# Six edits to an ordered one-core kernel: loaded keys, another bank for a scale, earlier state adds, later settling, blank rows behind a relu

## The chip, the cores and the metric

The kernel runs on one core of a Trainium2 chip. The metric is the device time in microseconds of one execution, as the median of several runs. A core has TensorE (PE, matrix products), VectorE (DVE), ScalarE (ACT), GpSimd (POOL) and SyncE (SP), each with a queue of its own in program order, and 16 DMA engines that move data between DRAM and the on-chip memory. On-chip data lie in SBUF; TensorE writes into the banks of PSUM.

## The reference

An attention with a decaying state, whose output rows go through a layer of experts. B, H, S, D = 4, 8, 768, 48; the layer has 3072 tokens of width 384, 8 experts and a hidden width of 1024.

```python
for t in range(S):
    kt, vt, rt = k[:, :, t], v[:, :, t], r[:, :, t]
    cur = einsum('bhd,bhe->bhde', u[None] * kt, vt)
    y[:, :, t] = einsum('bhd,bhde->bhe', rt, state + cur)
    state = w[None, :, :, None] * state + einsum('bhd,bhe->bhde', kt, vt)
x = y.transpose(0, 2, 1, 3).reshape(B * S, H * D)

logits = x @ w_gate + modality_bias[modality_id]
e_idx = argmax(logits, axis=1)
probs = softmax(logits)
for e in range(8):
    mask = e_idx == e
    h = maximum(x[mask] @ w1[e], 0)
    out[mask] = probs[mask, e] * (h @ w2[e])
```

## The kernel before

**Units and steps.** The sequence is cut into 6 chunks of 128 tokens; a chunk of one batch is a unit, 24 in all. Step i of a loop computes the scores of unit i+1, the values of unit i and the tail of unit i-1 (its scaling, its split into two float16 halves, its transposition). The order of every engine's instructions is the order in which the program emits them: nothing reorders them later, so a line that is moved in `run` moves its instructions on each engine that they use.

**One unit.** `turned` loads the transposed receptance of a unit into a tile `ud`, and its transposed keys behind it unless the unit is in `TURNED`; `lines` loads keys and values by rows into `kv`. For units of `TURNED`, `keys_turned` makes the transposed keys on TensorE, with four transposes into a PSUM bank `pkT`. `decay` (GpSimd, `rc`) and `keys` (VectorE, `kc`) multiply both by powers of the decay. `scores` multiplies kc by rc into two banks, `causal` masks these into `at`, and `values` writes the unit's output into the bank `py` and its new state into the bank `pst`. Also in `pst` stands the bonus of the next unit: `taken` copies it out (`d`), and `own` multiplies it by the values (`dv`, eight ScalarE instructions in two halves, `own(i, 0)` and `own(i, 1)`). `add` adds dv to the output, and `token` does this and squares the sum on ScalarE. `state` adds the bank's new state to the decayed state in SBUF (two VectorE adds); the decay itself is `fade` on ScalarE, or for units 4 to 13 a matmul with a diagonal matrix, L497, and two copies by `settled_state`. From step `EASED` = 15 on, VectorE does `taken`; units from 17 on are in `OWNED` and take their bonus by a VectorE reduction over products instead.

**Routing.** Tokens are routed by groups of units, (0,4), (4,8), (8,12), (12,16), (16,19), (19,22), (22,24). For each there are `logits` (a PSUM bank `pr`), `choose`, `count`, `place`, and `send`, which writes token rows to DRAM by expert. `choose`, `place` and `ahead` (the numbers of the next early blocks, called settling below) are generators: they wait in a list `fills`, and `fill()` emits one small operation, `fill(99)` all that are left. `route(i, d, f)` calls f for the group whose last unit is i - d; `SOON` = 8 parts the first two groups from the later ones.

**Early expert blocks.** The weights of the expert that comes first are loaded during steps 8 and on; `norm` squares a sixth on ScalarE, and `scales` sums the squares with a small matmul into a free corner of some bank and works out a power of two. Nine blocks of 128 rows (slots 0 to 8) of this expert run between the steps and after them: `s_turn` reads the rows transposed from DRAM, `s_up`, `s_high`, `s_low`, `s_down` are the two layers with the relu between them, `s_take` and `s_give` write the result out. Behind them the job part takes the other blocks one after another: `turn` reads a block's rows transposed into `mxT` (or `xn`, from which VectorE copies), `up` is the first layer.

**Blank rows.** `pads` writes 128 blank rows behind an expert's rows, at a place that SyncE first loads into a register, one write of 193 KB for each. `pace` makes SyncE load a value and so wait until it is there.

Of the kernel before, what the change touches and what calls it, by code (L numbers as in the profile page):

```python
# [19 lines left out]
B, H, S, D = 4, 8, 768, 48  # L20
# [3 lines left out]
DM = H * D  # L24
# [3 lines left out]
FB = F // P  # L28
# [15 lines left out]
DENSE = 6  # L44
FADED = range(4, 14)
SHARED = range(9, 14)
TURNED = range(1, 15)
RAISED = range(6, 12)
OWNED = range(17, 24)
GROUPED = 6  # L50
EASED = 15
# [4 lines left out]
SOON = 8  # L56
GROUPS = ((0, 4), (4, 8), (8, 12), (12, 16), (16, 19), (19, 22), (22, 24))
# [10 lines left out]
class _Kernel:  # L68
# [260 lines left out]
    def turned(self, i):  # L329
# [3 lines left out]
        ud = self.ud[i % len(self.ud)]  # L333
        m = n if i in TURNED else 2 * n
        self.nc.sync.dma_start(ud[LOW:TOP, :m], self.pd[b * NCH + c].rearrange("j d n -> (j d) n")[:, :m])
# [12 lines left out]
    def keys_turned(self, i):  # L348

        if i in TURNED:  # L350
            u = self.ctx_[i]
# [620 lines left out]
    def norm(self, junk, q):  # L972
        self.nc.scalar.activation(junk, self.raw[:, q * WQ : (q + 1) * WQ], AF.Square, accum_out=self.ssq[:, q : q + 1])
# [191 lines left out]
    def run(self):  # L1165
# [22 lines left out]
        groups = {}  # L1188
        fills = []
        at, begin, mid = {}, {}, {}  # L1190

        def plan(step, f):
            at.setdefault(step, []).append(f)
# [12 lines left out]
        def scales(key, q, bank):  # L1206
            for _ in self.scales_(key, slice(q, q + 1), bank):
                pass
# [15 lines left out]
        O = GROUPS[0][1] + 4  # L1224
# [7 lines left out]
            plan(O + 9 + q, norm(q))  # L1232
        for q in range(3):
            plan(O - 1 + q, norm(q))
        begin[O + 2] = lambda: scales("w1", 0, self.ctx_[O + 1]["py"][:, DM + H :])
        for q in range(3):
            plan(O + 2 + q, wide(q))
            plan(O + 2 + q, norm(3 + q))
# [9 lines left out]
        def route(i, d, f, *args):  # L1248
            for lo, hi in GROUPS:
                if hi - 1 + d == i and lo in groups:  # L1250
                    f(groups[lo], *args)

        def each(i, *fs):
            for f in fs:
                if live(i):
                    f(i)


        def fill(n=1):
            while n and fills:  # L1260
                g = fills.pop(0)
                if next(g, fills) is not fills:
                    fills.append(g)
                    n -= 1

        for i in range(NU - 1):
# [27 lines left out]
            if i and i < EASED:  # L1294
                self.taken(i)
                self.shared(i)
            self.token(i - 1) if i else None
            if ups.get(i - 2) is not None:
                self.s_take(ups[i - 2])
# [2 lines left out]
            if i >= EASED:  # L1302
                self.taken(i)
                self.shared(i)
                for j in range(2):
                    self.state(i - 1, j)
            fill()
            if 0 < i < NU - 5:
                self.pace(self.ctx_[i]["d"])
                each(i + 5, self.turned)  # L1310
# [38 lines left out]
            if i - 2 in RAISED:  # L1349
                self.flipped(i - 2)  # L1350
            mid.get(i, lambda: None)()
            for j in range(2):
                each(i + 1, lambda i: self.causal(i, j))
                if j == 0:
                    each(i - 1, self.low)
                fill()
            self.own(i, 1)
            if late:
                for d in (6, 7):
                    route(i, d, lambda u: (self.rest(self.ctx_[i]["dv"][:1, DM - 1 :]), self.send(u, 1)))  # L1360
# [22 lines left out]
            if down is not None:  # L1383
                self.s_down(down, 0)
                self.s_down(down, 1)
            if i != O + 4 and any(hi - 1 + d == i for lo, hi in GROUPS for d in (4, 5)):
                fill(99)
            route(i, 2, lambda u: u["lo"] >= SOON and self.logits(u))
            route(i, 4, lambda u: u["lo"] >= SOON and self.count(u))
# [8 lines left out]
        i, j = NU - 2, NU - 1  # L1398
# [79 lines left out]
        self.s_low(7, 0)  # L1478
        self.s_up(7, 1)

        self.pads(*range(E - 2))
        self.turn(0, self.s_row(NE), m2, group="first")
        self.pads(E - 2, E - 1)
        self.s_high(7, 1)
        run(jobs, 5)
        self.s_low(7, 1)
        run(jobs, 4)
# [119 lines left out]
```

## Time and profile before

| | us |
|---|---|
| median of 3 runs | 337.85 |
| lowest, highest | 337.64, 340.84 |
| profiled execution | 340.3 |
| its span | 338.0 |

The span goes from the first to the last instruction of the profiled execution, and the execution's own time is 2.3 us longer. TensorE's granted clock is 0.996 of full speed over the span. Busy time is counted by engine; a matmul's weight load (PEld) runs beside other matmuls. In the trace steps 3 to 22 begin on TensorE with their scores; step 8 at 46.31, step 9 at 51.95, step 10 at 56.98, step 13 at 75.43, step 15 at 93.08, step 17 at 109.51. The job part begins at 192.58.

### The profile page before, as it was taken

To read this page: it belongs to the slowest core of one execution; us is meant where nothing else is said; L and a number is where in the kernel's file an instruction comes from. 1 tells how busy PE (TensorE), PEld (TensorE's weight loads), DVE (VectorE), ACT (ScalarE), POOL (GpSimd) and SP (SyncE) were. 2 spreads that over 40 slices of the span, in tenths; PEclk is the share of its full clock that TensorE was granted. 3 is DMA by queue.
4 is the path that set the end of the run, shared out by engine and by line. 5 is a ranking of instruction groups with operands and counts; after the bars stand their busy time and mean duration, and the time that the engine had idled before them with its cause. 6 is when DMAs were issued, how large, how long until landed. Compare 5 with 4: busy or idle time off the path is not lost. (4 is left out here: it accounts for less than half of the span.)

```text
span 338.0 us, 15234 instructions
## 1 busy us (share of the span) xinstructions
PE 320.1 (95%) x5450; PEld 263.6 (78%) x5450; DVE 213.7 (63%) x727; ACT 181.5 (54%) x500; POOL 160.5 (47%) x241
## 2 busy tenths in 40 slices
PE   6998999999999999999998999999999999999993
PEld 3787989888787879698876788886888777777771
DVE  7879867899989887976685423386333332333950
ACT  7898689899465757567411222274222225542920
POOL 8978764997489857562557112103111111111211
PEclk9999999999999999999999999999999999999998
DMA  6799797995499999964336532119622111122120
GB/s 187 238 162 185 140 234 227 337 233 173 72 215 239 275 244 303 268 107 120 93 113 239 124 70 47 47 47 327 121 64 53 47 47 23 47 64 53 37 47 5
DMA packets 58014, 47.93 MB, mean 142 GB/s; under 512 B 42345, under 2 KB 50808, under 8 KB 57713
## 3 DMA queue, kind: packets, MB, share of 16 engines
q1 hardware_dynamic: 54768, 37.85, 50.2%
q0 software_dynamic: 3200, 9.47, 7.6%
q8 instruction: 30, 0.49, 0.6%
q14 instruction: 16, 0.12, 0.1%
HBM read 27.21 MB, written 11.83 MB: 116 GB/s over the span
## 5 line engine op out<-in xcount | busy, mean ns | idle before, releaser
L1067 PEld LDWEIGHTS <-whi 128*128 128x128 f16 x1248 | 72.6, 98 | 3.2
L1076 DVE SCALAR_TENSOR_TENSOR hl<-phb,hh 128x256 f16<-128x256 f32 (+1 forms) x48 | 24.6, 512 | 68.8 <-issue 39.2
L1130 PEld LDWEIGHTS <-hh 128*128 128x128 f16 x416 | 39.0, 98 | 29.1 <-ACT hh L1071 3.5
L1067 PE MATMUL phb<-mxT,whi 128*128 128x128 f16 x768 | 50.9, 219 | 0.0
L1071 ACT ACTIVATE hh<-phb 128x256 f16<-128x256 f32 (+1 forms) x48 | 21.5, 455 | 40.6 <-PE phb L1067 21.0
L438 ACT ACTIVATE dv<-kv,d 128x48 f32<-128x48 f32 x172 | 42.9, 324 | 0.0
L1067 PEld LDWEIGHTS <-wlo 128*128 128x128 f16 x624 | 37.7, 98 | 0.0
L1036 POOL TENSOR_TENSOR seenb<-otb,putb 128x1 int32<-128x1 int32 x16 | 4.1, 256 | 64.8 <-ACTq L1538 51.7
L458 DVE TENSOR_TENSOR at<-psc,mask 128x512 f32<-128x512 f32 x48 | 32.5, 682 | 1.0 <-PE psc L452 0.9
L1130 PEld LDWEIGHTS <-hl 128*128 128x128 f16 x208 | 19.8, 98 | 15.7 <-issue 2.5
L366 POOL TENSOR_TENSOR rc<-ud,powr 112x512 f32<-112x512 f32 (+1 forms) x25 | 30.9, 1240 | 0.2
L1130 PE MATMUL po<-whi,hh 128*128 128x384 f16 x136 | 27.7, 326 | 2.0 <-ACT hh L1071 1.2
L1067 PE MATMUL phb<-mxT,wlo 128*128 128x128 f16 x384 | 29.3, 219 | 0.0
L701 POOL DMA_INDIRECT rows<-row,posi x24 | 24.6, 1024 | 9.8 <-issue 3.4
L452 PE MATMUL psc<-rc,kc 64*64 64x128 f32 (+1 forms) x768 | 27.9, 276 | 1.4 <-POOL rc L366 1.1
L1130 PE MATMUL po<-whi,hl 128*128 128x384 f16 x136 | 28.0, 326 | 1.2 <-PEq L1603 0.7
L1130 PE MATMUL po<-wlo,hh 128*128 128x384 f16 x136 | 27.7, 326 | 0.0
L1027 ACT ACTIVATE otb<-po,fac 128x384 f32<-128x384 f32 x16 | 9.3, 580 | 34.0 <-PE phb L1067 31.4
L1067 PE MATMUL phs<-mxT,whi 128*128 128x128 f16 x432 | 27.1, 219 | 0.1
L489 PE MATMUL py<-kv,at 128*64 128x48 f32 x768 | 26.6, 222 | 0.0
L489 PEld LDWEIGHTS py<-kv,at 128*64 128x64 f32 x768 | 25.2, 138 | 0.8 <-issue 0.5
L1009 DVE SCALAR_TENSOR_TENSOR wlo<-raw,ws,whi 128x1024 f16<-128x1024 f32 (+1 forms) x20 | 24.9, 1269 | 1.2 <-issue 0.7
(294 smaller groups left out, 623.0 us busy)
## 6 DMA issues: line engine op xcount, KB each, us to landing
kv<-in_pt SPq DMA_DIRECT2D x21, 384.0 KB
ud<-in_pd SPq DMA_DIRECT2D x10, 384.0 KB
raw<-in_w SPq DMA_DIRECT2D x12, 256.0 KB
raw<-in_w SPq DMA_DIRECT2D x6, 512.0 KB
raw<-in_w SPq DMA_DIRECT2D x2, 1536.0 KB, 7.1
ud<-in_pd SPq DMA_DIRECT2D x14, 192.0 KB
rows<-pad SPq DMA_DIRECT2D x10, 193.0 KB
rt<-in_pt SPq DMA_DIRECT2D x7, 192.0 KB
```

What stands on the lines that cost most here:

```text
L366: nc.gpsimd.tensor_mul(u["rc"][:TOP, s], u["rT"][:TOP, s], self.powr[:TOP, s])
L438: nc.scalar.activation(u["dv"][:, sl], u["v"][:, sl], AF.Copy, scale=u["d"][:, h : h + 1])
L452: nc.tensor.matmul(u["ps"][j][s, pr * P : (pr + 1) * P], u["kc"][r, pr, s], u["rc"][r, pr, :], start=True, stop=True)
L458: nc.vector.tensor_mul(u["at"][:, j * NPR : (j + 1) * NPR, :], u["ps"][j].rearrange("p (q t) -> p q t", q=NPR), self.mask.unsqueeze(1).to_ ...
L489: nc.tensor.matmul(py[t, sl], u["at"][:, j * NPR + pr, t], u["v"][:, sl], start=c == h == 0, stop=h == H - 1, skip_group_check=True)
L701: i = nc.gpsimd.indirect_dma_start(out=self.rows, out_offset=bass.IndirectOffsetOnAxis(ap=u["posi"][:, b : b + 1], axis=0), in_=u["row"][: ...
L1009: self.nc.vector.scalar_tensor_tensor(self.wlo[:, sl], self.raw[:, sl], sc, self.whi[:, sl], ALU.mult, ALU.subtract)
L1027: self.nc.scalar.activation(ot, po[:, :DM], AF.Copy, scale=gf[:, t : t + 1])
L1067: self.nc.tensor.matmul(ph[:, q * P : (q + 1) * P], w[:, c0 : c0 + P], self.xT[:, xq, t * P : (t + 1) * P], start=i == q == 0, stop=i == l ...
L1071: self.nc.scalar.activation(self.hh[:, f0 : f0 + fb, t * P : (t + 1) * P], p3, AF.Relu)
L1076: self.nc.vector.scalar_tensor_tensor(self.hl[:, f0 : f0 + fb, r], p3, 0.0, self.hh[:, f0 : f0 + fb, r], ALU.max, ALU.subtract)
L1130: self.nc.tensor.matmul(po[:, :DM], h[:, f, t * P : (t + 1) * P], w[:, c0 : c0 + DM], start=first, stop=last)
```

## The change

- Units 8 to 11 leave `TURNED`: their transposed keys come by DMA with the receptance, and TensorE doesn't transpose them.
- The first scale's matmul (before step 10's second half) writes into columns 480 and on of the second group's `pr`, not into unit 9's `py`.
- From step 15 on the state's adds are emitted ahead of `token`, `taken` and what stands between.
- What `fills` still holds for the groups from unit 8 on is emitted in the first half of steps 17 and 21, behind `fill()`, no longer at the ends of steps 16 and 20.
- `own(i, 1)` is emitted ahead of the masks, no longer behind them.
- The seventh slot's second relu is emitted ahead of seven of the blank rows' eight writes and of the job part's first transposing read, as is a `pace` on its result. (`pads(E)`, one more write, stays where it was.)

```diff
-TURNED = range(1, 15)
+TURNED = (*range(1, 8), *range(12, 15))
...
-        begin[O + 2] = lambda: scales("w1", 0, self.ctx_[O + 1]["py"][:, DM + H :])
+        begin[O + 2] = lambda: scales("w1", 0, groups[B]["pr"][:, 480:])
...
             if i and i < EASED:
                 self.taken(i)
                 self.shared(i)
+            if i >= EASED:
+                for j in range(2):
+                    self.state(i - 1, j)
             self.token(i - 1) if i else None
...
             if i >= EASED:
                 self.taken(i)
                 self.shared(i)
-                for j in range(2):
-                    self.state(i - 1, j)
             fill()
+            route(i, 6, lambda u: u["lo"] >= SOON and fill(99))
...
             mid.get(i, lambda: None)()
+            self.own(i, 1)
             for j in range(2):
                 each(i + 1, lambda i: self.causal(i, j))
                 if j == 0:
                     each(i - 1, self.low)
                 fill()
-            self.own(i, 1)
...
-            if i != O + 4 and any(hi - 1 + d == i for lo, hi in GROUPS for d in (4, 5)):
+            if i != O + 4 and any(hi - 1 + d == i for lo, hi in GROUPS for d in ((4,) if lo >= SOON else (4, 5))):
                 fill(99)
...
+        self.s_high(7, 1)
+        self.pace(self.hh[:, FB // 2, :2])
         self.pads(*range(E - 2))
         self.turn(0, self.s_row(NE), m2, group="first")
         self.pads(E - 2, E - 1)
-        self.s_high(7, 1)
```

## Rows read from the trace of the kernel before

**Rows 1.** The page, busy time, share of the span and instructions of each engine.

```profile
PE 320.1 (95%) x5450; PEld 263.6 (78%) x5450; DVE 213.7 (63%) x727; ACT 181.5 (54%) x500; POOL 160.5 (47%) x241
```

**Rows 2.** Busy time by stretch; last columns granted clock, DMA share, GB/s.

```profile
48.29:60.65 12.36, 11.82 (x317) 10.96 (x316) 8.97 (x33) 12.21 (x41) 7.13 (x8) 1.00 0.84 274
...
46.00:55.00 9.00, 8.81 (x234) 8.12 (x233) 7.28 (x21) 8.14 (x26) 4.74 (x4) 1.00 1.06 268
75.43:85.42 9.99, 9.43 (x233) 9.01 (x231) 9.78 (x27) 9.70 (x21) 7.23 (x8) 1.00 0.70 185
```

**Rows 3.** Timeline of TensorE in step 7: start, us, engine, line, operation.

```profile
42.65 0.65 PE L354 MATMUL pkT<-id,kv 128*112 128x128 f32 x4
...
43.23 0.88 PE L482 MATMUL py<-st,rc 112*64 112x96 f32 x16
```

**Rows 4.** Timeline of ScalarE and TensorE, steps 8 and 9; idle time before in brackets.

```profile
48.29 1.06 ACT L973 ACTIVATE junk<-raw 128x1024 f16<-128x1024 f32 x1 [0.51 <-DMA raw<-in_w]
...
55.18 0.17 ACT L421 COPY d<-pst 128x8 f32<-128x8 f32 x1
...
55.53 0.57 PE L497 MATMUL pst<-st,wd 112*64 112x48 f32 x15
```

**Rows 5.** Groups by line and form, the decayed keys: busy us, mean ns.

```profile
L404 DVE TENSOR_TENSOR kc<-pkT,powk 112x512 f32<-112x512 f32 x14 | 9.6, 682 | 0.8 <-PE pkT L354 0.8
...
L404 DVE TENSOR_TENSOR kc<-ud,powk 112x512 f32<-112x512 f32 x9 | 7.9, 882 | 0.0
```

**Rows 6.** DMA issues, the loads of transposed keys and receptance.

```profile
ud<-in_pd SPq DMA_DIRECT2D x10, 384.0 KB
...
ud<-in_pd SPq DMA_DIRECT2D x14, 192.0 KB
```

**Rows 7.** Timeline around the first scale, step 10.

```profile
60.42 0.17 DVE L613 TENSOR_SCALAR pr<-sx 128x4 int32<-128x4 int32 x1 [0.28 <-PE pr L600]
60.45 0.20 ACT L529 ACTIVATION_READ_ACCUMULATOR row<-py 128x1 f32 x1
...
60.69 0.17 PE L988 MATMUL py<-wssq,onesb 128*128 128x3 bf16 x1 [0.58 <-ACT row L529]
```

**Rows 8.** Timeline of step 15: fade, state, and the next state's matmuls.

```profile
94.95 0.79 ACT L470 ACTIVATE st<-st,w 112x192 f32<-112x192 f32 x2
...
95.77 0.72 DVE L542 TENSOR_TENSOR st<-st,pst 64x192 f32<-64x192 f32 x2
...
96.63 0.64 PE L502 MATMUL pst<-kv,kt 128*64 128x48 f32 x16 [0.58 <-DVE st L542]
```

**Rows 9.** Timeline of step 17: last settling operation, state, the next state's matmuls.

```profile
111.19 0.15 DVE L831 TENSOR_SCALAR skip<-again 128x1 int32<-128x1 f32 x1
...
112.20 0.71 DVE L542 TENSOR_TENSOR st<-st,pst 64x192 f32<-64x192 f32 x2
...
113.06 0.64 PE L502 MATMUL pst<-kv,kt 128*64 128x48 f32 x16 [0.71 <-DVE st L542]
```

**Rows 10.** Timeline of the seventh slot's second half, and the job part's first matmuls.

```profile
178.38 0.83 PE L1067 MATMUL phs<-mxT,wlo 128*128 128x128 f16 x12
...
181.00 0.60 ACT L1071 ACTIVATE hh<-phs 128x512 f16<-128x512 f32 x1 [3.12 <-remote]
...
181.65 0.82 PE L1130 MATMUL pos<-whi,hh 128*128 128x384 f16 x4 [1.14 <-ACT hh L1071]
...
192.58 0.61 PE L1067 MATMUL pha<-mxT,whi 128*128 128x128 f16 x8
```

**Rows 11.** Timeline of SyncE's DMA queue: blank rows and first transposing read.

```profile
177.00 8.13 SPq L959 DMA_DIRECT2D rows<-pad  x7
187.46 1.26 SPq L1054 DMA_TRANSPOSE mxT<-rows  x1
```

**Rows 12.** Timeline: the next transposing read, and VectorE's copy of what it brought.

```profile
194.07 1.23 SPq L1054 DMA_TRANSPOSE xn<-rows  x1
...
197.69 0.36 DVE L1516 COPY mxT<-xn 128x768 f16<-128x768 f16 x1
```

## The prediction

> **What bounds the kernel now.** I read the page's busy times first, then the busy time by stretch, and then, for each edit, the timeline and the waits at its own place. TensorE is busy for 320.1 of 338.0 us [rows 1], so nothing that another engine saves counts unless TensorE waited for it. The rest of its time lies in short waits of 0.5 to 1.2 us, and each of the six edits can be held against one of them, or against none. In the stretch that the first edit touches the other engines are full as well: from 48.29 to 60.65 ScalarE is busy for 12.21 of 12.36 us, in step 13 VectorE for 9.78 and ScalarE for 9.70 of 9.99, and the DMA engines' share is 1.06 in 46 to 55 and 0.84 from 48.29 to 60.65 [rows 2]. So TensorE is not alone on the path there: what it saves, it soon waits for. I treat the parts as one sum, each beside the wait that it could remove.
>
> **Keys of units 8 to 11 loaded.** It removes four sets of four transposes. One set costs TensorE the time from its start at 42.65 to the next matmul at 43.23, 0.58 us [rows 3]: four sets are 2.3 us, the most that this edit can give. How much of it arrives is set by ScalarE. At 48.29 its norm waits 0.51 us for a weight piece from memory, so what TensorE saved in steps 6 and 7 doesn't bring ScalarE forward; from there ScalarE has no more than 0.15 us of idle time up to 60.65 [rows 2, 4]. In step 9 its copy out of the state bank ends at 55.18 + 0.17 = 55.35 and TensorE writes that bank from 55.53, 0.18 us behind [rows 4]. A TensorE that is more than 0.18 us sooner waits there. I take 0.18 + 0.15, so 0.3 us. From the other side, the decayed keys are then read from SBUF, at 882 ns where the PSUM form took 682 [rows 5]: 4 x 0.2 = 0.8 us on VectorE, which is 8.97 of 12.36 us busy in that stretch, so I cost it at nothing; were its cover gone, 0.8. The four loads grow from 192 to 384 KB [rows 6]: 0.79 MB more, at the 268 GB/s of the saturated stretch 2.9 us of transfer, issued in steps 3 to 6 ahead of the weight pieces that ScalarE waits for at 48.29. If all of that pushed the weight pieces, ScalarE's norms would be 2.9 us later [rows 2, 4]. I take none of it, because the loads go out five steps before they are needed and TensorE isn't among the readers of those pieces until step 10. Term: -0.3 us, bounds -2.3 and +2.9.
>
> **First scale in the logits' bank.** TensorE waits 0.58 us at 60.69 for ScalarE's square of unit 9, whose read of the accumulator ends at 60.45 + 0.20 = 60.65; the scale's matmul writes other columns of the same bank than the square reads. So what is waited for here is the bank, not the columns [rows 7]. In the new bank the last neighbour is VectorE's write of 60.42 + 0.17 = 60.59 [rows 7]. If the bank counts again, the matmul goes 0.06 us sooner; if columns alone counted, 0.58. I take 0.06, since the only row of such a pair shows the bank. The Trainium skill ("PSUM — Partial Sum Buffer", section "Terms") says that TensorE and another engine must not be in one bank and quadrant at the same time, whichever columns they use; the trace agrees in the old bank with its 0.58 us, and by this rule the edit gives 0.06 and not 0.58.
>
> **State sooner, in step 15.** TensorE waits 0.58 us at 96.63 for the state's two adds, 95.77 to 96.49. But these can't start before ScalarE's fade of the same state ends, at 94.95 + 0.79 = 95.74 [rows 8]. Putting them ahead of the output's add only lets the add wait in their place. With d v sooner the fade itself could come sooner, so the bounds are 0 and -0.58; I take 0, because d v and fade are the same work of the same engine in either order.
>
> **State sooner and settling later, in step 17.** Here no fade is in the way. VectorE does the settling's operations until 111.19 + 0.15 = 111.34, then the output's add and the reduction, 0.86 us together, and only then the state (112.20, 0.71), and TensorE waits 0.71 us for it at 113.06 [rows 9]. With the flush moved behind the state, and the state ahead of add and reduction, the adds come at least that 0.86 us sooner, which is more than the wait, and the wait goes. What the settling now holds up is the keys of step 19, behind which nothing of step 17 waits. Term: -0.71, bounds -0.71 and 0.
>
> **Blank rows behind the relu.** The seventh slot's second relu starts at 181.00, though TensorE's last matmul into its bank ends at 178.38 + 0.83 = 179.21; TensorE waits 1.14 us for it at 181.65 [rows 10]. Ahead of it SyncE had sent blank rows: seven issues in 8.13 us from 177.00 [rows 11]; by sevenths one takes 1.16 us, by the six steps between them 1.36. What holds the relu isn't named by a wait (its releaser is given as remote). If the blank rows' writes are the reason, the change gives the 1.14 back, and TensorE is ready for the job part's first matmul at 192.58 - 1.14 = 191.44 [rows 10]. But SyncE now waits for the relu, and six blank rows, the transposing read and the rest of its queue go behind it. With the relu's end at 180.0: six times 1.16 is 6.97, so 187.0; the read went out 187.46 - 185.13 = 2.33 us behind the last blank row's issue, so 189.3 [rows 11]; a read of this kind takes from 194.07 to 197.69, 3.62 us, until its data are used [rows 12], so 192.9. By six times 1.36 it is 194.1. Before, the read had 192.58 - 187.46 - 3.62 = 1.5 us to spare; now it comes 0.3 to 1.5 us after the old time. So the wait of 1.14 us is not given back: a later read takes its place. I take the middle, +0.9. If the read stood no longer behind its blank rows, -1.14; if the relu is at 181.6 as before, 1.6 more, +1.9 to +3.1.
>
> **The sum.** -0.3 - 0.06 + 0 - 0.71 + 0.9 = -0.17 us. Against the profiled execution, 340.3 us with a span of 338.0, that is 340.1; that execution is 2.4 us over the median of the runs, 337.85, and I carry the difference over to the median: 337.7.
>
> **Rivals.** First, the transposes are worth what they cost. For it: TensorE is the busiest engine, and ScalarE's idle time counts only up to 60.65. Against it: steps 9 and 13 [rows 2, 4]. -2.3 instead of -0.3 makes -2.2 in all and 335.7; with the read also free, -4.2 and 333.6.
>
> Second, on the other side, the relu is late for a reason of its own, and the blank rows are in series with it. For it: the releaser is remote, no row names the blank rows, and a write of 193 KB to DRAM has no consumer on ScalarE. Against it: the lateness falls just where they are sent [rows 10, 11]. It decides, against a sum of -0.17, as soon as the relu ends 0.2 us after the 180.0 taken above; at 181.6 the sum is -0.3 - 0.77 + 2.5 = +1.4, so 339.3. The Trainium skill ("Runtime: NRT & Kernel Launch", section "Instruction fetch mechanics") calls the crossing of a block of instructions mostly hidden; by that the relu wouldn't be late through code loading, and the first reading would stand. No row here decides it.
>
> Third, the greater key loads push the weight pieces: for it, the DMA engines are full between 46 and 55; against it, the loads go out in steps 3 to 6, ahead of that stretch, and the share over 48.29 to 60.65 is 0.84. +2.9 - 0.77 + 0.9 = +3.0, so 340.9; together with the second rival 342.5.
>
> Fourth, the change doesn't do what it says in step 17, and the settling holds VectorE at another place of the same path: 0 for -0.71, so 338.4. For it: the flush is as long as before. Against it: the keys that follow it aren't needed in step 17.
>
> **How the numbers follow.** Forecast 0.50 (own range 336.4 to 339.0), first rival 0.20, second 0.14, third 0.10, fourth 0.06. A measurement here can tell about 1%, 3.4 us, from no change: so the line lies at 334.5 and 341.2. Half of the first rival lies below, 0.10 faster. Of the second and third their sum lies past 341.2, and the third with the noise of a run: 0.08 slower; 0.82 remain between. The range goes from 334.6 to 340.9, which takes in the third rival's full price and leaves out some 0.10 on either side.
>
> **What would show it.** Right: in the changed profile the step at 61 still shows a wait of about 0.5 us before the scale's matmul, now by VectorE; step 9 shows a new wait of the state bank by ScalarE; step 17 has no wait for the state; the second relu starts before 180.0 and the job part's first matmul waits for the transposing read. Wrong: no new wait in steps 9 to 13 (then the first rival); a relu still a microsecond behind its bank (the second); a weight piece awaited for more than 0.51 us at the norm (the third). What would make the forecast wrong altogether is a stall that moves: the waits named remote or issue in this profile have no cause that a row shows, and each is as long as any term of the sum.

## The result and the profile after

The changed kernel takes 338.92 us (median of 22 runs, 337.05 to 342.58); the kernel before took 337.64 beside it (22 runs, 335.12 to 340.84). The ratio is 1.0052, with a 95% interval from 1.0029 to 1.0074: 1.0 to 2.5 us slower. The forecast was 337.7 against 337.85, a gain of 0.17 us. The time lies inside the range, but it moved the other way.

The spans of the two profiled executions are nearly the same, 338.2 and 338.0 us, and a comparison of spans alone would say that nothing happened. The timeline of the changed kernel says otherwise. First the page's busy times, which answer to [rows 1]:

```profile
PE 319.4 (94%) x5434; PEld 263.1 (78%) x5434; DVE 214.0 (63%) x727; ACT 181.7 (54%) x500; POOL 159.7 (47%) x241
```

TensorE has 16 matmuls less and is busy for 0.7 us less, although a group of matmuls that runs slower, shown below, takes back 1.5 us. The places of the small edits, from timelines of TensorE and VectorE (start, duration, engine, line, operation, idle time before it and what ended that):

```profile
60.89 0.17 DVE L613 TENSOR_SCALAR pr<-sx 128x4 int32<-128x4 int32 x1 [1.25 <-PE pr L600]
...
61.12 0.18 PE L988 MATMUL pr<-wssq,onesb 128*128 128x3 bf16 x1 [0.26 <-DVE off L825]
...
97.54 0.64 PE L502 MATMUL pst<-kv,kt 128*64 128x48 f32 x16 [0.59 <-DVE d L421]
...
111.51 0.71 DVE L542 TENSOR_TENSOR st<-st,pst 64x192 f32<-64x192 f32 x2
...
113.04 0.63 PE L502 MATMUL pst<-kv,kt 128*64 128x48 f32 x16
```

The scale still waits, now for VectorE, 0.26 us for 0.58 [rows 7]; VectorE's write into the new bank ends 0.06 us before the matmul. In step 15 the wait of 0.58 for the state [rows 8] is one of 0.59 for the copy of `taken`, which now stands behind the state. In step 17 the state is done by 112.22 and the wait of 0.71 us [rows 9] is gone. At the seventh slot TensorE is 0.89 us ahead of before; how much of this is the edits' doing, one profile can't tell. The end of the slots, from one timeline of the changed kernel, to be held against [rows 10 to 12]:

```profile
177.48 0.83 PE L1067 MATMUL phs<-mxT,wlo 128*128 128x128 f16 x12
...
178.41 0.60 ACT L1071 ACTIVATE hh<-phs 128x512 f16<-128x512 f32 x1 [1.47 <-PE phs L1067]
...
179.88 6.35 SPq L959 DMA_DIRECT2D rows<-pad  x6
...
188.41 1.26 SPq L1054 DMA_TRANSPOSE mxT<-rows  x1
...
192.93 2.30 PE L1067 MATMUL pha<-mxT,whi 128*128 128x128 f16 x23 [2.39 <-DMA mxT<-rows]
```

(The relu goes ahead of eight of the nine blank rows' writes, six in front of the read and two behind it. `pads(E)`, the first of the seven in [rows 11], stays ahead of it.) In this execution the relu is on time and TensorE doesn't wait for it. But the six blank rows go out behind it, the read behind these, and TensorE, done with the slots at 190.54, stands still for 2.39 us. There is a second price, in the busy times by stretch (us, then busy us and instructions of PE, PEld, DVE, ACT and POOL, granted clock, DMA share, GB/s). First the changed kernel:

```profile
190.54:192.93 2.39, 0.00 (x1) 0.00 (x0) 0.00 (x0) 0.58 (x1) 1.03 (x2) 1.00 0.33 94
192.93:196.48 3.55, 3.55 (x37) 3.55 (x37) 0.27 (x2) 0.00 (x0) 0.15 (x1) 0.55 0.54 162
196.48:198.59 2.11, 2.11 (x40) 2.11 (x37) 1.18 (x6) 0.98 (x2) 0.00 (x0) 0.94 0.07 8
```

and the same matmuls in the kernel before:

```profile
192.58:194.62 2.04, 2.04 (x40) 2.04 (x37) 0.02 (x1) 0.58 (x1) 0.52 (x2) 1.00 0.27 97
```

The first group of the job part takes 3.55 us for 2.04: behind the wait the granted clock is 0.55 over that stretch, mostly the lower of its two levels (1.2 GHz for 2.4). So against before the seat of the loss is here: 0.89 us ahead at the start of the slot's second half, 2.21 ahead after the relu that wasn't late, 0.35 behind at the job part's first matmul, 1.96 behind at its second layer.

That the spans still agree is this execution's doing. Further on, TensorE waits three times for ScalarE in the kernel before:

```profile
229.29 0.82 PE L1130 MATMUL po<-whi,hh 128*128 128x384 f16 x4 [0.61 <-ACT hh L1071]
...
286.44 0.82 PE L1130 MATMUL po<-whi,hh 128*128 128x384 f16 x4 [0.78 <-ACTq L1538]
...
319.31 0.82 PE L1130 MATMUL po<-whi,hh 128*128 128x384 f16 x4 [0.61 <-ACT hh L1071]
```

The same three waits, of 0.61, 0.75 to 0.84 and 0.61 us, stand in all twelve profiles of the experiments, a second one of the changed kernel (E10) among them. In this first one none of them is longer than 0.25 us, so of the 1.96 us only 0.3 are left at the end. It is no typical execution.

The other loss of this profile is early. TensorE's timeline in steps 5 to 8 shows four idle times that name no releaser:

```profile
35.95 0.46 PE L413 MATMUL pst<-uw,rk 112*64 112x2 f32 x10 [0.49 <-issue]
...
41.33 0.24 PE L497 MATMUL pst<-st,wd 112*48 112x48 f32 x1 [1.01 <-issue]
...
46.45 0.25 PE L497 MATMUL pst<-st,wd 112*64 112x48 f32 x2 [0.85 <-issue]
...
52.10 0.32 PE L489 MATMUL py<-kv,at 128*64 128x48 f32 x4 [1.21 <-issue]
```

Together 3.56 us; step 9 begins 1.74 us later than before, step 13 still 0.69 later and step 17 0.87 later.

### The profile page after: what moved, and what is told of

The parts are those of the page before. It is cut to its first block, busy times and chain, and to the rows that moved or that the text cites. A ratio compares the mean times of both kernels' runs of the same rounds, so it can differ in the third digit from the quotient of the medians.

```text
span 338.2 us, 15203 instructions
## 1 busy us (share of the span) xinstructions
PE 319.4 (94%) x5434; PEld 263.1 (78%) x5434; DVE 214.0 (63%) x727; ACT 181.7 (54%) x500; POOL 159.7 (47%) x241
## 5 line engine op out<-in xcount | busy, mean ns | idle before, releaser
L1067 PEld LDWEIGHTS <-whi 128*128 128x128 f16 x1248 | 73.6, 99 | 5.8 <-issue 3.0
```

Source lines behind the costliest of these rows:

```text
L1067: self.nc.tensor.matmul(ph[:, q * P : (q + 1) * P], w[:, c0 : c0 + P], self.xT[:, xq, t * P : (t + 1) * P], start=i == q == 0, stop=i == l ...
```

## The experiments

Each has a ratio to the kernel before, run beside it on the same chip. E1 to E4 ran together, then E5 to E8, then E9 to E12.

**E1: the loaded keys alone.**

```diff
-TURNED = range(1, 15)
+TURNED = (*range(1, 8), *range(12, 15))
```

> The kernel before with the loaded keys of units 8 to 11 as its only edit. Theory: the 0.79 MB more of loads delay the blocks of TensorE's own instructions, which come by DMA too; in the changed kernel TensorE stood idle for 0.49, 1.01, 0.85 and 1.21 us at matmuls 727, 855, 982 and 1110 of its stream, some 128 apart, with a 16 KB instruction packet ending 1.3 to 1.5 us before each. Then this kernel shows such waits in steps 5 to 9 and step 10 begins 1 to 2 us later than before; the time is 1.003 to 1.006 of before. Rival: TensorE's four transposes saved (0.58 us each) count, and the waits in the changed kernel came from the other edits; then step 10 begins 0.3 to 2.3 us sooner and the time is 0.993 to 0.999.

Measured: 1.0013 (0.9980 to 1.0047). The idle times are there (1.01 us at matmul 727, 1.13 at 1110, 0.2 to 0.4 at 855, 1237 and 1364), and step 10 begins 0.65 us later, less than the 1 to 2 expected; the time doesn't show it. The theory's place was right, and its loss isn't confirmed: the interval holds no change as well as most of the loss. Of the rival's range, a gain of 0.3% and more is outside the interval; a smaller one isn't.

**E2: the blank rows alone.**

```diff
+        self.s_high(7, 1)
+        self.pace(self.hh[:, FB // 2, :2])
         self.pads(*range(E - 2))
         self.turn(0, self.s_row(NE), m2, group="first")
         self.pads(E - 2, E - 1)
-        self.s_high(7, 1)
```

> The kernel before with only the blank rows and the first transposing read behind the seventh slot's second relu. Theory: the relu is 1.3 us sooner, the job part's first matmul waits 2 to 3 us for the read, and TensorE's granted clock falls to the lower level in the 3 us after that wait, which costs 1.5 us more; together 2.5 to 3 us at the job part's second step and 1.007 to 1.009 of before. Rival: the read was late only through the other edits (TensorE was 0.9 us ahead there); then the wait is under 1.5 us, the clock stays at 1.00 and the time is 0.999 to 1.002.

Measured: 1.0108 (1.0065 to 1.0150), the greatest effect of all parts. Its timeline:

```profile
177.83 0.83 PE L1067 MATMUL phs<-mxT,wlo 128*128 128x128 f16 x12
...
180.37 0.60 ACT L1071 ACTIVATE hh<-phs 128x512 f16<-128x512 f32 x1 [3.03 <-remote]
...
181.02 0.82 PE L1130 MATMUL pos<-whi,hh 128*128 128x384 f16 x4 [1.06 <-ACT hh L1071]
...
181.84 6.33 SPq L959 DMA_DIRECT2D rows<-pad  x6
...
191.06 1.26 SPq L1054 DMA_TRANSPOSE mxT<-rows  x1
...
193.95 1.50 PE L1067 MATMUL pha<-mxT,whi 128*128 128x128 f16 x24 [1.83 <-DMA mxT<-rows]
```

The relu is as late as before (1.06 us of TensorE's time, for 1.14 [rows 10]), though no blank row of these six has gone out when it starts. So these rows weren't what held it: both waits stand in this profile, one behind the other. The clock stays at 1.00 behind the wait of 1.83 us (busy time by stretch, as above):

```profile
193.95:195.98 2.03, 2.03 (x37) 2.03 (x37) 0.27 (x2) 0.00 (x0) 0.71 (x1) 1.00 0.61 215
```

Of my expectation only the time came out, not the relu, the length of the wait or the clock. The profile shows less than the time does: its execution is the fastest of the six (341.77 us; median 344.46), and it is only 1.4 us behind the profile before at the end.

**E3: the other four edits** (the two parts above undone in the changed kernel).

> The kernel before with the other four edits: the scale in the logits' bank, the state sooner, settling later, d v sooner. Theory: step 17's wait of 0.71 us goes and the scale's of 0.58 shrinks to 0.3 or less; the seventh slot begins about 1 us sooner, 0.996 to 0.998 of before. Rival: the settling's work waits elsewhere on the same path, and the time is 0.999 to 1.001.

Measured: 0.9977 (0.9952 to 1.0002), -0.8 us with an interval that just reaches 1. The sum of these terms in the prediction was -0.77 us. In its profile the scale's wait is 0.31 us and step 17's wait is gone, but the seventh slot begins only 0.30 us sooner than before, where I had expected 1. A second run is E12.

**E4: the loads without their use.**

```diff
-        m = n if i in TURNED else 2 * n
+        m = n if i in TURNED and i not in range(8, 12) else 2 * n
```

> The kernel before, in which units 8 to 11 load their transposed keys as well, but still transpose them on TensorE and read the transposed ones; nothing reads the loaded ones. TensorE's stream is that of before, instruction for instruction. Theory (late instruction blocks through the DMA traffic): idle times of 0.4 to 1.2 us without a releaser some 128 matmuls apart between 30 and 60 us, step 10 begins 1.5 to 4 us later, and the time is 1.004 to 1.011 of before. Rival one (the place of the block borders in the stream counts, which the removed transposes shift): no such waits, the time within 0.1% of before. Rival two (readers of the loaded keys wait, GpSimd above all): the waits of TensorE name GpSimd or a load.

Measured: 0.9999 (0.9962 to 1.0036). Its profile shows one such idle time:

```profile
36.30 0.46 PE L413 MATMUL pst<-uw,rk 112*64 112x2 f32 x10 [1.10 <-issue]
```

It stands at matmul 727, where E1 and the changed kernel have theirs, and no wait names a reader of the loaded keys. So the greater loads seem to bring it alone, which speaks against both rivals; it is one idle time in one profile. The time misses the theory's 1.004 to 1.011: 0.79 MB of loads cost nothing that can be measured. Some 2 us behind this idle time TensorE's granted clock fell, so the profile's times by step aren't used:

```profile
38.50:49.00 10.50, 10.50 (x179) 9.79 (x178) 6.40 (x23) 5.22 (x22) 4.62 (x8) 0.52 1.15 255
```

**E5: the read behind the third blank row.**

```diff
-        self.pads(*range(E - 2))
+        self.pads(*range(E - 5))
         self.turn(0, self.s_row(NE), m2, group="first")
-        self.pads(E - 2, E - 1)
+        self.pads(*range(E - 5, E))
```

> The changed kernel with the job part's first transposing read behind the third blank row of the seven that follow the relu, and the other five behind the read. Theory (the read is late because six blank rows and the landing of the last stand ahead of it): the read goes out some 3 us sooner, at 184.6 to 185.5, bound by the landing of the third blank row and of the last routed rows (184.6); the job part's first matmul has no wait over 0.3 us, TensorE's clock stays at 1.00 there, and the time is 0.986 to 0.991 of the changed kernel, 0.991 to 0.997 of before. Rival: the second read, for the next job, is now late by as much, since five blank rows stand ahead of it; then the wait moves to the first matmul behind the first job's second layer and the time is 1.000 to 1.006 of before.

Measured: 0.9989 (0.9955 to 1.0023). Timeline:

```profile
183.56 2.85 SPq L959 DMA_DIRECT2D rows<-pad  x3
...
188.35 1.30 SPq L1054 DMA_TRANSPOSE mxT<-rows  x1
...
191.07 4.81 SPq L959 DMA_DIRECT2D rows<-pad  x5
...
193.51 1.50 PE L1067 MATMUL pha<-mxT,whi 128*128 128x128 f16 x24
...
197.67 1.25 SPq L1054 DMA_TRANSPOSE xn<-rows  x1
...
201.46 0.90 PE L1130 MATMUL po<-whi,hl 128*128 128x384 f16 x4 [0.50 <-DVE mt L1519]
```

The first read goes out 5.8 us behind the relu's end (9.4 in the changed kernel), and the job part starts without a wait: the theory's half. The second read now has five blank rows ahead of it, and TensorE waits 0.50 us for what it brought: the rival's half, smaller than its full size. The loss of the changed kernel is mostly gone, the gain isn't there.

**E6: the changed kernel without the blank rows' edit.**

> The changed kernel with the blank rows, the read and the relu in the order of before; the other five edits stay. Theory (the blank rows' place makes the whole loss, the state and settling a small gain, the keys nothing): 0.996 to 1.001 of before. Rival (the loaded keys cost 1 to 2 us through late instruction blocks): 1.002 to 1.005.

Measured: 0.9953 (0.9924 to 0.9983), faster than before, and a little better than the theory's 0.996. Idle times without a releaser in steps 7 and 8 are 0.56 and 0.22 us here.

**E7: neither transposes nor greater loads.**

```diff
-        m = n if i in TURNED else 2 * n
+        m = n if i in TURNED or i in range(8, 12) else 2 * n
...
-        self.ctx_.setdefault(i, {}).update( rT=ud[:, :n].rearrange("p (a t) -> p a t", a=NPR), kT=ud[:, n:].rearrange("p (a t) -> p a t", a=NPR))
+        self.ctx_.setdefault(i, {}).update( rT=ud[:, :n].rearrange("p (a t) -> p a t", a=NPR), kT=(ud[:, :n] if i in range(8, 12) else ud[:, n:]).rearrange("p (a t) -> p a t", a=NPR))
```

(besides E1's edit)

> The kernel before without the transposes of units 8 to 11 and without the greater loads: those units take the transposed receptance in the place of the keys, so their keys are left out of the result. It gives the worth of the transposes alone. Theory of the prediction (ScalarE is full there, so little arrives): 0.998 to 1.001 of before. Rival (TensorE's 2.3 us count, and the loads had eaten them): 0.992 to 0.995.

Measured: 0.9977 (0.9951 to 1.0002), between the two. The trace speaks for the prediction's reading: with the transposes away and nothing in their place, TensorE waits for ScalarE's copy out of the state bank, as it nowhere does in the kernel before:

```profile
43.76 0.61 PE L497 MATMUL pst<-st,wd 112*64 112x48 f32 x15 [0.63 <-ACT d L421]
...
54.27 0.61 PE L497 MATMUL pst<-st,wd 112*64 112x48 f32 x15 [0.30 <-ACT d L421]
```

The transposes taken away stood in steps 6 to 9 (from 37.36 to 53.6 in the trace before). At the beginning of step 6 this kernel is 0.84 us ahead of before, at that of step 10 1.22: of 2.3 us it gains some 0.4. No idle time without a releaser of 0.2 us or more stands between 30 and 62 us.

**E8: the clock held.**

```diff
+        hold = self.ps_r.tile([P, 512], F32, tag="r", name="hold")
+        for _ in range(10):
+            nc.tensor.matmul(hold, self.ones16, self.warm, start=True, stop=True)
         self.up("a", lambda: next(once, lambda: None)())
```

> The changed kernel with ten matmuls of 512 columns of ones, which nothing reads, ahead of the job part's first matmul, in the time in which TensorE waits for the transposing read. Theory: the read is as late as in the changed kernel, but TensorE's clock stays at 1.00 behind the wait, and the second group of the first layer begins 1.3 to 1.6 us sooner than there; 0.995 to 0.997 of the changed kernel. Rival (the matmuls behind the wait are slow because of their weights or the data's arrival, not by the clock): as slow as there, 1.000 of the changed kernel.

Measured: 1.0045 (1.0008 to 1.0082). The timeline:

```profile
191.90 2.32 PE L1517 MATMUL hold<-warm 128*128 128x512 f16 x10
194.31 1.50 PE L1067 MATMUL pha<-mxT,whi 128*128 128x128 f16 x24
```

and the busy time by stretch behind the ten matmuls:

```profile
194.31:196.35 2.04, 2.04 (x38) 2.04 (x38) 0.28 (x2) 0.00 (x0) 0.30 (x1) 1.00 0.79 283
```

The clock stays at 1.00 and the group takes 2.04 us as before; so what made it 3.55 in the changed kernel was the clock. In the time this is no saving that can be measured (the changed kernel itself has 1.0052 and, in E10, 1.0045): TensorE still stands 2.41 us at the place (191.90 to 194.31), and the ten matmuls themselves end only at 194.2.

**E9: the wait without the queue behind it.**

```diff
+        self.pads(*range(E - 2))
         self.s_high(7, 1)
         self.pace(self.hh[:, FB // 2, :2])
-        self.pads(*range(E - 2))
         self.turn(0, self.s_row(NE), m2, group="first")
```

> The changed kernel with the first six blank rows back ahead of the relu; SyncE's wait for the relu stays, with only the transposing read and two blank rows behind it. Theory (not the wait, but the six blank rows that queue behind it make the read late): SyncE passes the relu at about 181 to 182 and then still waits for the landing of the sixth blank row, so the read goes out as in the kernel before, the job part's first matmul has no wait, and the time is that of the kernel without the blank rows' edit, 0.993 to 0.998 of before. Rival (the wait itself costs, by what it holds up on SyncE): 1.002 to 1.008.

Measured: 0.9953 (0.9915 to 0.9992), as E6. Timeline:

```profile
178.57 0.60 ACT L1071 ACTIVATE hh<-phs 128x512 f16<-128x512 f32 x1 [3.13 <-remote]
...
179.22 0.82 PE L1130 MATMUL pos<-whi,hh 128*128 128x384 f16 x4 [1.11 <-ACT hh L1071]
...
185.25 1.26 SPq L1054 DMA_TRANSPOSE mxT<-rows  x1
...
190.15 1.50 PE L1067 MATMUL pha<-mxT,whi 128*128 128x128 f16 x24
```

SyncE waits for the same relu, which is as late as ever; the read goes out 6.03 us behind TensorE's restart at 179.22, where E2's takes 10.04 (181.02 to 191.06), and nobody waits for it. The wait costs nothing that can be measured. The six rows behind it do.

**E10: the changed kernel again.**

> The changed kernel once more, beside its variants. Theory: 1.004 to 1.008 of before, and a second profile of it shows again a wait of the job part's first matmul for the read of 1.8 us or more. Whether the relu is late in it (a wait of TensorE of some 1.1 us, as in eight of ten profiles so far) and whether TensorE's clock falls behind the wait differ from execution to execution. Rival: its first profile was no typical one, and there is no wait for the read.

Measured: 1.0045 (1.0011 to 1.0079). Its timeline:

```profile
178.01 0.83 PE L1067 MATMUL phs<-mxT,wlo 128*128 128x128 f16 x12
...
180.56 0.60 ACT L1071 ACTIVATE hh<-phs 128x512 f16<-128x512 f32 x1 [3.06 <-remote]
...
181.22 0.82 PE L1130 MATMUL pos<-whi,hh 128*128 128x384 f16 x4 [1.07 <-ACT hh L1071]
...
182.04 6.33 SPq L959 DMA_DIRECT2D rows<-pad  x6
...
190.43 1.26 SPq L1054 DMA_TRANSPOSE mxT<-rows  x1
...
195.09 2.72 PE L1067 MATMUL pha<-mxT,whi 128*128 128x128 f16 x24 [2.79 <-DMA mxT<-rows]
```

and the busy time by stretch behind that wait, and behind an idle time of 1.31 us that ended at 37.11:

```profile
195.09:198.61 3.52, 3.52 (x38) 3.52 (x37) 0.27 (x2) 0.00 (x0) 0.00 (x0) 0.55 0.40 126
...
37.11:41.00 3.89, 3.89 (x80) 3.53 (x81) 2.43 (x7) 2.83 (x13) 2.38 (x5) 0.59 1.16 195
```

Here everything comes together: the late relu (1.07), the late read (2.79), the clock (3.52 us for 2.04). From 0.44 us ahead of the profile before it falls to 3.99 behind, and it stays there to the end (4.1 us).

**E11: as E6.**

> The changed kernel without the blank rows' edit, a second time, beside the next. Theory: 0.993 to 0.998 of before; between 30 and 60 us TensorE again has idle times without a releaser near matmuls 727, 855, 982 or 1110, as in all six profiles with the greater loads so far, and of another length than before.

Measured: 0.9971 (0.9934 to 1.0007); idle times without a releaser of 0.30 us each at matmuls 982 and 1110.

**E12: as E3.**

> The same without the loaded keys as well, a second time: scale, state, settling and d v alone. Theory (the loaded keys give and take as much): the time within 0.2% of the run before this one, and idle times without a releaser of no more than 0.3 us each between 30 and 60 us. Rival (the keys are worth their transposes): 0.3 to 0.7% above the run before this one.

Measured: 0.9986 (0.9954 to 1.0018), 0.15% above E11; one idle time in step 8 is 0.38 us, more than expected. With E3 and E6, 0.24% apart the same way, and E1, 0.13% the other way, the loaded keys are worth nothing that these runs can tell.

## Why the prediction was wrong

**The step that failed is the blank rows' term: +0.9 us, with the relu's end taken at 180.0 and the clock left out; measured +2.5 to +3.6.** E2 alone gives 1.0108, 3.6 us with an interval of 2.2 to 5.1; E10 against E11, on one chip, 1.0045 / 0.9971 = 1.0074, 2.5 us, and against E9 1.0092, 3.1 us. (Each of these two quotients is uncertain by about 1.7 us either way, an estimate from the intervals of the runs in it.) With the six rows ahead of the relu the same kernel is faster than before (E6 0.9953, E9 0.9953) or as fast (E11 0.9971, with an interval that holds 1), so this part turned a small gain into the loss. That the time lies inside the range all the same is the width of the range, not the merit of this term. Two things made it too small, the relu's lateness and the clock; the chain behind the relu came out.

First, its starting point. I took the relu's end at 180.0, as if the blank rows' writes had held it. E2 sends none of the six until the relu is done, and it is late all the same. In 12 of 14 profiles of this study TensorE waits 1.06 to 1.19 us for this relu, with the blank rows ahead (before, E1, E6, E9) or behind it (E2, E8, E10); in E5 it is 0.42, in the changed kernel's first profile 0. E8 and E10 are instruction for instruction the changed kernel up to there, and in them it is late: what differs is the execution, not the program. So the 1.14 us that the forecast counted as won back is mostly not won, and the second rival had it right: blank rows in series behind a relu that is late for a reason of its own. Its price, +1.9 to +3.1, holds the smaller of the two measurements.

Second, the clock, which was in no term: behind a wait of 2.39 us, and of 2.79 in E10, the next group of matmuls runs at a mean of 0.55 of full speed and takes 1.5 us more. Behind 1.83 us (E2) it doesn't. E8, with matmuls in the gap and the clock at 1.00, speaks for the idle time as the reason. The profiles show this price; the times don't part it from the rest, since E8 is no faster than E10, which ran on another chip.

The chain from the relu's end to the job part's first matmul is what the forecast had: 12.9 to 14.1 us, measured 13.92 in the changed kernel's first profile, 13.93 in E10 and 12.98 in E2. Its parts differ and make up for each other: 0.9 us from the relu's end to the first row's issue, which I had left out; 6.33 to 6.35 us for the six rows (I had 6.97 to 8.1); 2.06 to 2.89 to the read (2.33); 2.89 to 4.66 from there to the first matmul (3.62). And since SyncE waits for a relu that waits for TensorE, the chain moves with TensorE, so the gains ahead of it were rightly added. In the first profile the relu is in time and TensorE 0.89 us ahead; the first matmul comes 0.35 behind, so the part costs 1.24 us there, inside the 0.3 to 1.5 of the forecast. With the relu late it is 1.37 + 0.55 = 1.92 us in E2 and 2.51 + 0.37 = 2.88 in E10, inside the second rival's 1.9 to 3.1. The clock comes on top.

The mechanism of the term, a later read that takes the relu's place, was the forecast's, and E5 and E9 show it from both sides: with the read moved ahead of the last rows the job part starts without a wait, and with the rows ahead of SyncE's wait nothing is lost.

**Keys of units 8 to 11: small as predicted, wrong in the danger.** -0.3 us predicted; the runs give between +0.13% and -0.24%, too coarse to tell -0.3 from nothing. The first rival's -2.3 us, 0.7%, is outside E1's interval. The ScalarE wait that I had named as the reason stands in E7 and, with 0.63 and 0.30 us, in E8; in neither profile of the changed kernel. The third rival, that the loads push the weight pieces, isn't seen: in the changed kernel ScalarE waits for none of them between 20 and 62 us. What the loads do is another thing. In the nine profiles with the greater loads TensorE's idle times without a releaser between 30 and 62 us sum to 0.4 to 4.0 us, 1.7 in the mean; in the five without them to 0 to 0.8, 0.3 in the mean. The longer ones stand some 128 matmuls apart, at the same places of the stream in several kernels (727, 855, 982, 1110). In the changed kernel a packet of the instruction queue ends 1.5 us before the idle time at 41.33 does; the DMA view of 38.8 to 39.9, queue by queue (packets, MB, share):

```profile
q1 hardware_dynamic: 537, 0.16, 215.6%
q8 instruction: 1, 0.02, 5.6%
```

That TensorE's next instructions were in this packet, which went late among the loads' packets, is how I read it; the order of packets was not changed alone in any run, so this stays argued. The Trainium skill ("Runtime: NRT & Kernel Launch", section "Instruction fetch mechanics") says that TensorE's instructions come by DMA in blocks of 16 KB and that the crossing into a new block is mostly hidden. The packet agrees in its size, 0.02 MB. If my reading is right, the crossing isn't hidden in this stretch, with 0.49 to 1.21 us four times. In the time of the kernel these waits don't show (E1, E4).

**Scale, state and settling: the waits came out as argued.** Predicted -0.06, 0 and -0.71, together -0.77; E3 and E12 give 0.9977 and 0.9986, -0.8 and -0.5 us, which agrees, but each has an interval that holds 1. The scale's wait is 0.26 to 0.58 us in the new bank (0.26 here, 0.58 in E11), and names VectorE; that it shrinks at times by more than 0.06 I had left out. In step 15 another operation of VectorE took the state's place, as argued; it is the copy of `taken`, where I had named the output's add. In step 17 the wait is gone.

**What stays open:** why the seventh slot's second relu is late. TensorE's semaphore for it is recorded 1.84 to 1.98 us after the start of the matmul that raises it, in the twelve profiles in which it is over a microsecond late, and 0.23 after it in the changed kernel's first. No run here separates what holds it. One write, that of `pads(E)`, goes out ahead of the relu in every run; a kernel without the blank rows at all wasn't tried. Nor is it known why the first profile has neither this wait nor the three of the job part.

## What to carry to other kernels

A wait that is put into a queue is priced by what stands behind it on that queue up to the next thing that the busiest engine needs, and not by itself: here the wait was free (E9) and six short writes behind it cost 1%. Ask too what starts the queue: here it starts with the busiest engine's own work, so the transfer moved with that engine and the gains ahead of it could be added. A longer wait can cost the clock besides. And when a stall names no releaser, move the work that you suspect before you explain it: one run with the suspected work out of the way (E2) would have shown that the relu was late without it.

## What the runs showed of the hardware

The price of an idle TensorE isn't only the idle time: behind 2.39 and 2.79 us without work the granted clock was 0.55 over the next 3.5 us, and in E10 behind 1.31 us it was 0.59 over 3.89 us. The length of the wait alone doesn't decide it: behind 1.83 us in E2 the clock stayed at 1.00, and so it did behind the seventh slot's relu, 1.06 to 1.19 us in twelve profiles; in E4 it fell to 0.52 behind 1.10 us, and in E6 behind 1.18 us at 76.09:

```profile
76.10:79.50 3.40, 3.40 (x56) 3.32 (x57) 3.26 (x16) 3.12 (x11) 2.39 (x4) 0.50 0.38 120
```

With ten matmuls on constant data in the gap it stayed at 1.00 (E8, one profile).

Executions of one and the same program differ by more than the edits of this study are worth: the first profile of the changed kernel has 3.6 us of nameless idle time in steps 5 to 8 and a relu in time, the second has 1.3 us of it and the relu 1.07 us late. Their spans are 338.2 and 342.1 us. A single profile shows where a loss can stand; how much of it is paid on the whole, only the ratio over many runs tells.
